# A retention layer's products with its state, in whole-array form and in four 64x64 tiles

## The chip, the cores and the metric

The kernel runs on one core of one Trainium2 chip. The metric is the time of one execution on the device in microseconds (us), as the median of several runs. A profile is taken of one more execution; it has its own span, from the first to the last instruction.

The engines of the core are named as in the profile: PE is TensorE (matrix products; PEld is its loading of weights, the operand that stays in the array), DVE is VectorE, ACT is ScalarE, POOL is GpSimd, SP is SyncE, which starts transfers. PE writes to PSUM alone, an accumulator memory of eight banks, each of 512 float32 in each of 128 partitions.

## The reference

Two layers follow each other. The first is a recurrent retention layer over `q`, `k`, `v` of 4 batches, 8 heads, 768 tokens and a head size of 64; its result, with the heads side by side, is `x` of 3072 tokens by 512. The second is a feed-forward layer with a snake activation.

```python
gamma = 1.0 - 2.0 ** (-5.0 - np.arange(H))
for t in range(S):
    state = gamma[None, :, None, None] * state + np.einsum('bhd,bhe->bhde', k[:, :, t], v[:, :, t])
    y[:, :, t] = scale * np.einsum('bhd,bhde->bhe', q[:, :, t], state)

h = x @ w_in                                  # 3072x512 by 512x2048
g = h + np.sin(alpha * h) ** 2 / (alpha + 1e-09)
out = g @ w_out                               # 2048x512
```

## The kernel before

**Chunks.** The recurrence is computed in chunks of 128 tokens, six for each batch, 24 in all (`order`; first the four first chunks of the batches, then the others batch by batch). With the decay folded into the values (`scale_v`) and into a factor at the exit (`qg`), a chunk `j` needs, for each head: the scores of its tokens with each other, masked (`scores`, the mask on DVE); the mix, masked scores times values; the product of the queries with the state that the earlier chunks left (`inter`); and the sum of keys times values over its tokens, which is added to the state.

**Wide chunks.** Chunks from the second batch's third on (`wide`, L86, 14 of them) are laid out in another way: 64 tokens of four heads in partitions 0 to 63, the same 64 tokens of the other four heads in partitions 64 to 127, and two such halves `f` of a chunk. `load_seq` (L89) loads them, one transfer a head, into `qk_seq` and `v_seq`, and SP turns queries and keys (`turn`, a transposing transfer) into `qkT`, where a pair of heads lies in the two halves of the partitions.

**A burst.** `burst(old, new, first)` (L398) puts the attention work of two chunks on PE in one go: `inter(old)`, `scores(new)`, `mix(old)` with the sums. The program is recorded in the order in which it is written, engine by engine; there is no scheduler. PE's matmuls are named in the profile with the part of the array that they use, rows * columns: 128*128 is the whole array, 64*64 a quarter. Row halves of a quarter tile belong to the partitions of the operands, column halves to the partitions of the output. In the code `tiles4` goes over the four pairs of halves (b, e).

- `inter` (L321 to 329): four matmuls in whole-array form. The state lies in `s_bd`, for each pair of heads a 128x128 matrix with the two heads' 64x64 states on its diagonal and zeros beside them. The results start two banks, `py[0]` (tag ps) and `py[1]` (tag ty).
- `scores` (L331 to 347): 16 quarter-tile matmuls, in four groups of four, into the two banks of `pa`, columns 0 to 383 of each; then DVE multiplies by the mask into `aTw`.
- `mix` (L349 to 358): 16 quarter-tile matmuls that add to `py`, columns 0 to 255.
- the sums (L359 to 369): 16 quarter-tile matmuls into columns 256 to 383 of `py`. At a batch's last chunk the sums are those of the next batch's first chunk instead (8 matmuls over 128 rows, 128*64), and after the very last chunk there are none.

What the banks hold is taken out one slot later: `leave` (L375, the exit, `py` times `qg` into `xT`), `keep` (L380, the sums added to the float32 state `s_f`) on DVE, and `hand` (L388), which copies `s_f` into the diagonal of the next chunk's `s_bd`, by two copies of 64 partitions, on ACT or (last batch) POOL. Two `s_bd` take turns.

**The feed-forward work around it.** `phase` (L545) goes through a group of two chunks in eight slots: eight matmuls of the hidden layer (L425, 256 columns), ACT's sine and square, then the attention work that is set for this slot, then four output matmuls of the group before (L450, 512 columns), then DVE's `gT` (L440). A burst stands in every fourth slot. PSUM's four banks with tag mm hold hidden and output sums.

**Before the wide chunks.** Chunks of the first batch and the first two of the second use `stage_A`, `stage_M`, `stage_S` with whole rows; `keep_S` (L283) copies the state from `ps` into `s_bd` on ACT. The state before the first wide chunk comes this way too, and `into_sum` (L719) copies it into `s_f` on DVE. `later_tables` (L189) makes the tables of decay for the wide layout at the start, from `lgq`, the heads' log decay by place.

Of the kernel before, what the change touches and what calls it, by code (L numbers as in the profile page):

```python
# [8 lines left out]
F32 = mybir.dt.float32  # L9
BF16 = mybir.dt.bfloat16  # L10
ACTF = mybir.ActivationFunctionType
ALU = mybir.AluOpType


@with_exitstack
def kernel(
# [15 lines left out]
    nc = tc.nc  # L32
    B, H, S, D = q.shape
    C = 128
    NCH = S // C
    NJ = B * NCH
    NP = H // 2
# [15 lines left out]
    place = {j: (g, i) for g, js in enumerate(groups) for i, j in enumerate(js)}  # L53

    consts = ctx.enter_context(tc.tile_pool(name="consts", bufs=1))
    big = ctx.enter_context(tc.tile_pool(name="big", bufs=1))
    work = ctx.enter_context(tc.tile_pool(name="work", bufs=2))
    psum = ctx.enter_context(tc.tile_pool(name="psum", bufs=1, space=bass.MemoryType.PSUM))
# [8 lines left out]
    raw = {}  # L67
# [18 lines left out]
    def wide(j):  # L86
        return j >= NCH + 2 and j % NCH > 0

    def load_seq(bt, names="qkv"):  # L89

        cs = [c for c in range(NCH) if wide(bt * NCH + c)]
        nh = 2 * len(cs)
        if "q" in names:
            raw["seq", bt] = (big.tile([128, nh, 2, NP, D], BF16, name=f"qk_seq{bt}"),
                              big.tile([128, nh, NP, D], BF16, name=f"v_seq{bt}"))
        tqk, tv = raw["seq", bt]
        for name, src in (("q", q), ("k", k), ("v", v)):
            if name not in names:
                continue
            for h in range(H):  # L100
                r = slice(64 * (h // NP), 64 * (h // NP) + 64)
                o = tv[r, :, h % NP, :] if name == "v" else tqk[r, :, "qk".index(name), h % NP, :]
                nc.gpsimd.dma_start(out=o, in_=src[bt, h, cs[0] * C:, :].rearrange("(f i) d -> i f d", i=64))  # L103
        for i, c in enumerate(cs):
            j, f = bt * NCH + c, slice(2 * i, 2 * i + 2)
            raw["qk", j], raw["k", j], raw["v", j] = tqk[:, f], tqk[:, f, 1], tv[:, f]
# [54 lines left out]
    lg = consts.tile([128, H], F32, name="lg")  # L161
# [24 lines left out]
    lgq = consts.tile([128, NP], F32, name="lgq")  # L186
    maskq = consts.tile([128, 192], BF16, name="maskq")

    def later_tables():  # L189
        for b in range(2):  # L190
            r = slice(64 * b, 64 * b + 64)
            for f in range(2):
                nc.vector.tensor_scalar_add(tok[r, :, f], pos[r, :], float(64 * (f - b)))
            nc.vector.tensor_copy(lgq[r], lg[r, NP * b:NP * b + NP])
        for f in range(2):
            nc.vector.tensor_mul(expoq[:, :, NP * f:NP * f + NP],
                                 tok[:, :, f, None].to_broadcast([128, NCH, NP]),
                                 lgq[:, None, :].to_broadcast([128, NCH, NP]))
# [20 lines left out]
    s_bd = [big.tile([128, NP, 128], BF16, name=f"s_bd{i}") for i in range(2)]  # L219


    s_f = big.tile([128, NP, D], F32, name="s_f")


    st = {}
# [46 lines left out]
    def stage_S(j):  # L272
# [7 lines left out]
                                 start=(c == 0 and p == 0), stop=True, skip_group_check=True)  # L280
        return ps

    def keep_S(j, ps):  # L283
        for e in range(2):
            r = slice(64 * e, 64 * e + 64)
            nc.scalar.copy(s_bd[(j % NCH + 1) % 2][r, :, r], ps[r, :, :])  # L286
# [29 lines left out]
    def half(x):  # L316
        return slice(64 * x, 64 * x + 64)

    tiles4 = [(b, e) for b in range(2) for e in range(2)]

    def inter(j):  # L321

        qkT, s = st["qkT", j], s_bd[j % NCH % 2]
        st["py", j] = [psum.tile([128, 512], F32, name=f"py{b}", tag=tag) for b, tag in enumerate(("ps", "ty"))]
        for m in range(2):
            for b in range(2):
                nc.tensor.matmul(st["py", j][b][:, m * 128:(m + 1) * 128].rearrange("p (f i) -> p f i", f=2),  # L327
                                 s[:, 2 * b + m, :], qkT[:, m:m + 5:4, half(b)],
                                 start=(m == 0), stop=True, skip_group_check=True)

    def scores(j):  # L331

        qkT = st["qkT", j]
        pa = psum.tile([128, 2, 512], F32, name="pa", tag="pa")
        for m in range(2):
            for b, e in tiles4:
                nc.tensor.matmul(pa[half(b), e, 192 * m:192 * m + 128].rearrange("p (f i) -> p f i", f=2),  # L337
                                 qkT[half(e), 2 + m, half(b)], qkT[half(e), m:m + 5:4, half(b)],
                                 start=(m == 0), stop=True, skip_group_check=True)
            for b, e in tiles4:  # L340
                nc.tensor.matmul(pa[half(b), e, 192 * m + 128:192 * m + 192],
                                 qkT[half(e), 6 + m, half(b)], qkT[half(e), 4 + m, half(b)],
                                 start=False, stop=True, skip_group_check=True)
        aT = work.tile([128, 2, 2, 192], BF16, name="aTw", tag="aT", bufs=2)
        st["aT", j] = aT
        return {"mask": lambda: nc.vector.tensor_mul(aT, pa[:, :, 0:384].rearrange("p e (m t) -> p e m t", m=2),  # L346
                                                     maskq[:, None, None, :].to_broadcast([128, 2, 2, 192]))}

    def mix(j, first=None):  # L349

        py, aT, vs, c = st["py", j], st["aT", j], raw["v", j], j % NCH
        for m in range(2):
            for b, e in tiles4:
                nc.tensor.matmul(py[b][half(e), m * 128:(m + 1) * 128], vs[half(b), 0, 2 * m + e, :],  # L354
                                 aT[half(b), e, m, 0:128], start=False, stop=True, skip_group_check=True)
            for b, e in tiles4:
                nc.tensor.matmul(py[b][half(e), m * 128 + 64:(m + 1) * 128], vs[half(b), 1, 2 * m + e, :],
                                 aT[half(b), e, m, 128:192], start=False, stop=True, skip_group_check=True)
        now = j if c < NCH - 1 else first  # L359
        if now is not None:  # L360
            ks, vs = raw["k", now], raw["v", now]
            for f in range(2 if wide(now) else 1):
                for m in range(2):
                    for b, e in tiles4:
                        h = 4 * b + 2 * m + e
                        nc.tensor.matmul(py[b][half(e), 256 + 64 * m:320 + 64 * m],  # L366
                                         ks[half(b), f, 2 * m + e, :] if wide(now) else ks[:, h, :],
                                         vs[half(b), f, 2 * m + e, :] if wide(now) else vs[:, h, :],
                                         start=False, stop=True, skip_group_check=True)
        g, i = place[j]  # L370
        if g not in xT:
            xT[g] = work.tile([128, KS, sizes[g] * C], BF16, name="xT", tag="xT", bufs=3)
        x = xT[g][:, :, i * C:(i + 1) * C]

        def leave():  # L375
            for b in range(2):
                nc.vector.tensor_mul(x[:, 2 * b:2 * b + 2, :], py[b][:, 0:256].rearrange("p (m t) -> p m t", m=2),  # L377
                                     qg[:, c, 2 * b:2 * b + 2])

        def keep():  # L380
            for b in range(2):
                o, new = s_f[:, 2 * b:2 * b + 2], py[b][:, 256:384].rearrange("p (m d) -> p m d", m=2)
                if wide(now):
                    nc.vector.tensor_add(o, o, new)  # L384
                else:
                    nc.vector.tensor_copy(o, new)

        def hand():  # L388
            for e in range(2):
                copy = nc.gpsimd.tensor_copy if now // NCH == 3 else nc.scalar.copy  # L390
                copy(s_bd[(now % NCH + 1) % 2][half(e), :, half(e)], s_f[half(e)])  # L391

        more = {"exit": leave}
        if now is not None:
            more.update(keep=keep, hand=hand)
        return more

    def burst(old, new, first=None):  # L398

        inter(old)  # L400
        return {**(scores(new) if new is not None else {}), **mix(old, first)}

    def run(more, *kinds):
        for kind in kinds:
# [196 lines left out]
    b = early(1)  # L601
# [3 lines left out]
    c = early(3)  # L605
    a.sq("A")
    b.add()
    b = early(4, "ps")
# [8 lines left out]
    c = early(6)  # L617
    a.sq("A")
    b = early(7)
# [15 lines left out]
    b = Slot(0, 4, (n3, n4), 4)  # L635
# [4 lines left out]
    b = Slot(0, 10)  # L640
# [5 lines left out]
    b = Slot(0, 12)  # L646
# [5 lines left out]
    b = Slot(0, 14)  # L652
# [57 lines left out]
    for g in range(2, NG - 1):  # L710
        first = P.index(groups[g + 1][0])
# [5 lines left out]
        atts[place[0]].setdefault(place[1], []).append(fn)  # L717

    def into_sum():  # L719
        nc.vector.tensor_copy(s_f, st["ps"])  # L720

    def M_last(j):
        stage_M(j)
# [8 lines left out]
    for n in range(6, NJ + 1):  # L732
        new = P[n] if n < NJ else None
        first = new - 1 if n < NJ and new % NCH == 1 else None
# [46 lines left out]
```

## Time and profile before

| | |
|---|---|
| median of 3 runs | 214.4 us (214.4 to 214.45) |
| span of the profiled execution | 213.0 us |
| PE busy | 201.3 us, 94% of the span |
| PEld busy | 134.3 us, 63% |
| DVE busy | 155.1 us, 73% |
| ACT busy | 160.4 us, 75% |
| POOL busy | 107.2 us, 50% |
| granted clock of PE | 1.000 |

The page of the profile lists busy time, a chain of the work that ended last, followed back from the last instruction, and groups of instructions by line. A group's row has engine, operation, output <- inputs, the part of the array for PE, the shapes, how often, busy time in us and mean ns of one, and then the idle time of the engine just before them with what ended it. The timeline and the chain in order of time have the start and the length in us in their first two columns; instructions of one kind that follow each other are one row with their count. PE's matmuls are pipelined: several are in flight, and the length of one is its latency. "issue" is time in which an engine waited for nothing that the profile shows.

### The profile page before, as it was taken

The page shows a single profiled execution, that of the slowest core. Times are in us where ns is not written, and L with a number is a line of the kernel's source. Part 1 is how long each engine was busy: PE and PEld are TensorE (multiplying, and loading weights), DVE is VectorE, ACT ScalarE, POOL GpSimd, SP SyncE. Part 2 cuts the span into 40 slices and gives each one's busy share as a digit, 9 for nine tenths or more (in the row PEclk, how much of TensorE's full clock was granted, in tenths as well). Part 3 has the DMA queues.
Part 4 walks back from the last instruction along what each step waited for, and adds up shares of the span by engine and source line. Part 5 has one row for each costly group of instructions (what it writes and reads, how often), then busy time and mean ns, then how long its engine had stood idle before and what let it go on. Part 6 is the DMA issues. An engine that isn't in the chain of part 4 may idle for free.

```text
span 213.0 us, 5482 instructions
## 1 busy us (share of the span) xinstructions
PE 201.3 (94%) x2171; PEld 134.3 (63%) x2197; DVE 155.1 (73%) x349; ACT 160.4 (75%) x346; POOL 107.2 (50%) x145
## 2 busy tenths in 40 slices
PE   7898899899989999999999999999999999999994
PEld 3445554456766766766767667667667667666654
DVE  4877849876996678678678777777877877666550
ACT  7588696758887877977977977977876876788821
POOL 8976333787989729999789941001231131000000
DMA  9999999999998999999999994407403100110112
GB/s 128 155 196 187 206 207 170 149 114 241 142 158 74 147 160 150 159 103 152 167 151 170 150 145 104 98 3 98 103 12 91 51 30 23 52 49 0 52 49 99
DMA packets 101337, 25.00 MB, mean 117 GB/s; under 512 B 93872, under 2 KB 98368, under 8 KB 101312
## 3 DMA queue, kind: packets, MB, share of 16 engines
q0 software_dynamic: 77504, 13.38, 88.4%
q1 hardware_dynamic: 23664, 11.22, 27.0%
q8 instruction: 17, 0.28, 0.6%
q14 instruction: 8, 0.07, 0.1%
q10 hardware_dynamic: 144, 0.07, 0.1%
HBM read 27.27 MB, written 6.29 MB: 158 GB/s over the span
## 4 chain that ended last, share of the span: by engine, by line
PE 72%; DMA 13%; DVE 7%; POOL 5%; issue 2%; POOLq 0%
PE po L450 32%; PE ph L425 30%; DMA qkr<-in_k_dram 8%; DMA w_in<-in_moe_w_in_dram 4%; DVE gT L440 3%; DVE aT L269 2%; POOL qkr L83 2%; PE poh L475 2%; PE pa L337 2%; PE py L327 1%; POOL vr L83 1%; PE py L366 1%; PE py L354 1%; POOL w_out L116 1%; PE py L299 1%
## 5 line engine op out<-in xcount | busy, mean ns | idle before, releaser
L440 DVE SCALAR_TENSOR_TENSOR gT<-s,rec_alpha,ph 128x256 bf16<-128x256 f32 (+3 forms) x184 | 82.3, 488 | 37.8 <-ACT s L433 37.5
L428 ACT ACTIVATE s<-ph,alpha_sb 128x256 f32<-128x256 f32 (+3 forms) x184 | 79.1, 479 | 33.3 <-PE ph L425 31.7
L425 PE MATMUL ph<-xT,w_in 128*128 128x256 bf16 (+3 forms) x735 | 98.6, 277 | 0.3 <-DVE gT L440 0.2
L450 PE MATMUL po<-w_out,gT 128*128 128x512 bf16 x344 | 90.5, 380 | 4.3 <-issue 3.3
L425 PEld LDWEIGHTS <-w_in 128*128 128x128 bf16 x736 | 70.5, 98 | 30.7 <-issue 1.0
L433 ACT ACTIVATE s<-s 128x512 f32<-128x512 f32 (+1 forms) x92 | 57.1, 621 | 2.5
L450 PEld LDWEIGHTS <-gT 128*128 128x128 bf16 x368 | 33.8, 98 | 27.0 <-issue 1.2
L391 POOL CAST s_bd<-s_f 64x256 bf16<-64x256 f32 x10 | 3.9, 394 | 41.8 <-DVE s_f L384 23.6
L137 POOL TENSOR_TENSOR v_seq<-v_seq,kgq 128x512 bf16<-128x512 bf16 x14 | 14.7, 1081 | 10.5 <-ACT s L433 5.5
L103 POOL DMA_DIRECT2D qk_seq<-in_q_dram x24 | 17.1, 755 | 3.5 <-DMA v_seq<-in_v_dram 1.9
L103 POOL DMA_DIRECT2D qk_seq<-in_k_dram x24 | 17.0, 745 | 0.9 <-DMA qk_seq<-in_q_dram 0.5
L462 DVE COPY o_sb<-po 128x512 f32<-128x512 f32 x19 | 13.1, 691 | 5.4 <-PE po L450 5.4
L103 POOL DMA_DIRECT2D v_seq<-in_v_dram x24 | 17.0, 772 | 0.0
L346 DVE TENSOR_TENSOR aTw<-pa,maskq 128x768 bf16<-128x768 f32 x14 | 13.3, 950 | 0.0
L83 POOL DMA_DIRECT2D vr<-in_v_dram x10 | 9.2, 924 | 5.0 <-DMA w_in<-in_moe_w_in_dram 1.7
L494 PE MATMUL spare<-warm 128*128 128x512 bf16 x27 | 9.9, 492 | 1.3 <-DVE warm L156 1.2
L377 DVE TENSOR_TENSOR xT<-py,qg 128x256 bf16<-128x256 f32 x28 | 10.5, 416 | 0.0
L83 POOL DMA_DIRECT2D qkr<-in_q_dram x9 | 8.1, 902 | 3.7 <-DMA w_out<-in_moe_w_out_dram 1.6
L83 POOL DMA_DIRECT2D qkr<-in_k_dram x9 | 8.1, 897 | 3.7 <-DMA w_out<-in_moe_w_out_dram 3.3
L137 POOL TENSOR_TENSOR vr<-vr,kg 128x512 bf16<-128x512 bf16 x7 | 7.5, 1081 | 1.1 <-DMA vr<-in_v_dram 1.1
L269 DVE TENSOR_TENSOR aT<-pa,mask 128x1024 bf16<-128x1024 f32 x6 | 7.3, 1219 | 0.7 <-PE pa L265 0.7
L286 ACT CAST s_bd<-ps 64x256 bf16<-64x256 f32 x14 | 5.1, 361 | 2.3 <-PE ps L279 2.2
(93 smaller groups left out, 154.7 us busy)
## 6 DMA issues: line engine op xcount, KB each, us to landing
out_dram<-o_sb SPq DMA_DIRECT2D x23, 256.0 KB, 2.8
w_in<-in_moe_w_in_dram POOLq DMA_DIRECT2D x4, 512.0 KB, 10.6
w_out<-in_moe_w_out_dram POOLq DMA_DIRECT2D x4, 512.0 KB, 14.6
vr<-in_v_dram POOLq DMA_DIRECT2D x10, 128.0 KB, 6.5
qk_seq<-in_q_dram POOLq DMA_DIRECT2D x16, 80.0 KB, 6.3
qk_seq<-in_k_dram POOLq DMA_DIRECT2D x16, 80.0 KB, 4.6
v_seq<-in_v_dram POOLq DMA_DIRECT2D x16, 80.0 KB, 5.9
qkr<-in_q_dram POOLq DMA_DIRECT2D x9, 128.0 KB, 7.1
```

Source lines behind the costliest of these rows:

```text
L83: nc.gpsimd.dma_start(out=t, in_=chunk_of(src, j))
L103: nc.gpsimd.dma_start(out=o, in_=src[bt, h, cs[0] * C:, :].rearrange("(f i) d -> i f d", i=64))
L137: eng.tensor_mul(t, t, by[:, j % NCH, :, None].to_broadcast([128, H, D]))
L269: nc.vector.tensor_mul(aT.rearrange("p e n t -> p (e n) t"), pa.rearrange("p e n t -> p (e n) t"), m)
L346: return {"mask": lambda: nc.vector.tensor_mul(aT, pa[:, :, 0:384].rearrange("p e (m t) -> p e m t", m=2), maskq[:, None, None, :].to_broa ...
L377: nc.vector.tensor_mul(x[:, 2 * b:2 * b + 2, :], py[b][:, 0:256].rearrange("p (m t) -> p m t", m=2), qg[:, c, 2 * b:2 * b + 2])
L425: nc.tensor.matmul(self.ph[:, m, :], w_in[:, i, f * 128:(f + 1) * 128], xT[g][:, i, self.lo:self.hi], start=(m == 0 and i == 0), stop=(i = ...
L428: nc.scalar.activation(out=self.s[:, m, :], in_=self.ph[:, m, :], func=ACTF.Sin, scale=alpha_sb[:, f:f + 1])
L433: nc.scalar.activation(out=self.s, in_=self.s, func=ACTF.Square)
L440: nc.vector.scalar_tensor_tensor(gT[self.g][:, f, self.lo:self.hi], self.s[:, m, :], rec_alpha[:, f:f + 1], self.ph[:, m, :], op0=ALU.mult ...
L450: nc.tensor.matmul(po[g, ts], gT[g][:, f, ts * C:(ts + 1) * C], w_out[:, f, :], start=(f == 0), stop=(f == FF - 1))
L462: nc.vector.tensor_copy(o_sb, po[g, ts])
```

## The change

Two things change for the wide chunks.

First, `inter` uses quarter tiles. The state lies in `s_q`, without zeros: `s_q` has, in partition half e and place 2b + m, the state of one head. To let the eight products of a burst fall on four different tiles, the heads of the second half (4 to 7) are swapped in pairs (`spot`): in the loads, in the table `lgq`, in the output halves of `inter` and `mix` (`half(e ^ b)`) and in `sums`. `hand` becomes one copy of 128 partitions. Where the state comes from the old layout, `turned` copies it with the halves of heads 4 to 7 exchanged, by three copies.

Second, the sums of a chunk go ahead of the mix and into columns 384 to 511 of the scores' banks `pa`, where the next burst has scores (11 of 14 bursts). At the two batch borders they stay behind the mix in `py`. Ahead of the mix stands a wait for the last product of `inter`, written as a no-op with a dependency; in the built program the wait is on the mix's first weight load, or on an instruction of its own before it at the two batch borders, where that load has another wait already. PE's program has 112 instructions more (eight for each burst); ACT has 7 copies fewer, POOL 5 fewer, DVE 4 more.

```diff
+AFTER = mybir.DependencyInfo(mybir.DependencyClass.Sync, mybir.DependencyReason.DATA)
...
+    def spot(h):
+        return h // NP, (h % NP) ^ (h // NP)
...
             for h in range(H):
-                r = slice(64 * (h // NP), 64 * (h // NP) + 64)
-                o = tv[r, :, h % NP, :] if name == "v" else tqk[r, :, "qk".index(name), h % NP, :]
+                b, at = spot(h)
+                r = slice(64 * b, 64 * b + 64)
+                o = tv[r, :, at, :] if name == "v" else tqk[r, :, "qk".index(name), at, :]
...
-            nc.vector.tensor_copy(lgq[r], lg[r, NP * b:NP * b + NP])
+            for e in range(2):
+                nc.vector.tensor_copy(lgq[r, e::2], lg[r, NP * b + (e ^ b):NP * b + NP:2])
...
+    s_q = [big.tile([128, NP, D], BF16, name=f"s_q{i}") for i in range(2)]
...
+    def turned(to, ps, copy):
+        copy(to[:, 0:2], ps[:, 0:2])
+        for e in range(2):
+            copy(to[64 * e:64 * e + 64, 2:4], ps[64 - 64 * e:128 - 64 * e, 2:4])
+
     def keep_S(j, ps):
+        if wide(j + 1):
+            turned(s_q[(j % NCH + 1) % 2], ps, nc.scalar.copy)
+            return
...
     def inter(j):
-        qkT, s = st["qkT", j], s_bd[j % NCH % 2]
+        qkT, s = st["qkT", j], s_q[j % NCH % 2]
...
         for m in range(2):
-            for b in range(2):
-                nc.tensor.matmul(st["py", j][b][:, m * 128:(m + 1) * 128].rearrange("p (f i) -> p f i", f=2),
-                                 s[:, 2 * b + m, :], qkT[:, m:m + 5:4, half(b)],
-                                 start=(m == 0), stop=True, skip_group_check=True)
+            for b, e in tiles4:
+                last = nc.tensor.matmul(st["py", j][b][half(e ^ b), m * 128:(m + 1) * 128].rearrange("p (f i) -> p f i", f=2),
+                                        s[half(e), 2 * b + m, :], qkT[half(e), m:m + 5:4, half(b)],
+                                        start=(m == 0), stop=True, skip_group_check=True)
+        return last
...
+    def sums(now, to, lo):
+        ks, vs = raw["k", now], raw["v", now]
+        for f in range(2 if wide(now) else 1):
+            for m in range(2):
+                for b, e in tiles4:
+                    h = 4 * b + 2 * m + (e ^ b)
+                    nc.tensor.matmul(to[b][half(e), lo + 64 * m:lo + 64 + 64 * m],
+                                     ks[half(b), f, 2 * m + e, :] if wide(now) else ks[:, h, :],
+                                     vs[half(b), f, 2 * m + e, :] if wide(now) else vs[:, h, :],
+                                     start=False, stop=True, skip_group_check=True)
+
+    def mix(j, behind):
+        n = nc.tensor.nop()
+        tc.add_manual_dep(n.ins, behind.ins.name, AFTER)
+        py, aT, vs = st["py", j], st["aT", j], raw["v", j]
         for m in range(2):
...
+            for f in range(2):
+                for b, e in tiles4:
+                    nc.tensor.matmul(py[b][half(e ^ b), m * 128 + 64 * f:(m + 1) * 128], vs[half(b), f, 2 * m + e, :],
+                                     aT[half(b), e, m, 128 * f:128 + 64 * f],
+                                     start=False, stop=True, skip_group_check=True)
+
+    def burst(old, new, first=None):
+        c = old % NCH
+        behind = inter(old)
+        more = scores(new) if new is not None else {}
+        now = old if c < NCH - 1 else first
+        at = None
+        if now is old:
+            pa = st["pa", new]
+            at = [pa[:, b, 384:512] for b in range(2)]
+            sums(now, [pa[:, b] for b in range(2)], 384)
+        mix(old, behind)
+        py = st["py", old]
+        if now is not None and now is not old:
+            at = [py[b][:, 256:384] for b in range(2)]
+            sums(now, py, 256)
...
         def hand():
-            for e in range(2):
-                copy = nc.gpsimd.tensor_copy if now // NCH == 3 else nc.scalar.copy
-                copy(s_bd[(now % NCH + 1) % 2][half(e), :, half(e)], s_f[half(e)])
+            copy = nc.gpsimd.tensor_copy if now // NCH == 3 else nc.scalar.copy
+            copy(s_q[(now % NCH + 1) % 2], s_f)
...
     def into_sum():
-        nc.vector.tensor_copy(s_f, st["ps"])
+        turned(s_f, st["ps"], nc.vector.tensor_copy)
```

More of the change, by code (lines that the diff above doesn't have):

```diff
@@ L321, in inter @@
     def inter(j):
-        qkT, s = st["qkT", j], s_bd[j % NCH % 2]
+        qkT, s = st["qkT", j], s_q[j % NCH % 2]
         st["py", j] = [psum.tile([128, 512], F32, name=f"py{b}", tag=tag) for b, tag in enumerate(("ps", "ty"))]
         for m in range(2):
-            for b in range(2):
-                nc.tensor.matmul(st["py", j][b][:, m * 128:(m + 1) * 128].rearrange("p (f i) -> p f i", f=2),
-                                 s[:, 2 * b + m, :], qkT[:, m:m + 5:4, half(b)],
-                                 start=(m == 0), stop=True, skip_group_check=True)
+            for b, e in tiles4:
[3 more added lines that the diff above has]
+        return last
     def scores(j):
         qkT = st["qkT", j]
-        pa = psum.tile([128, 2, 512], F32, name="pa", tag="pa")
+        pa = st["pa", j] = psum.tile([128, 2, 512], F32, name="pa", tag="pa")
         for m in range(2):
@@ L347, in scores @@
                                                      maskq[:, None, None, :].to_broadcast([128, 2, 2, 192]))}
-    def mix(j, first=None):
-        py, aT, vs, c = st["py", j], st["aT", j], raw["v", j], j % NCH
-        for m in range(2):
[L353 to L370, printed above, removed]
@@ new lines, in burst @@
+    def burst(old, new, first=None):
[13 more added lines that the diff above has]
+            sums(now, py, 256)
+        g, i = place[old]
@@ L381, in keep @@
             for b in range(2):
-                o, new = s_f[:, 2 * b:2 * b + 2], py[b][:, 256:384].rearrange("p (m d) -> p m d", m=2)
+                o, add = s_f[:, 2 * b:2 * b + 2], at[b].rearrange("p (m d) -> p m d", m=2)
                 if wide(now):
-                    nc.vector.tensor_add(o, o, new)
+                    nc.vector.tensor_add(o, o, add)
                 else:
-                    nc.vector.tensor_copy(o, new)
+                    nc.vector.tensor_copy(o, add)
         def hand():
-            for e in range(2):
-                copy = nc.gpsimd.tensor_copy if now // NCH == 3 else nc.scalar.copy
-                copy(s_bd[(now % NCH + 1) % 2][half(e), :, half(e)], s_f[half(e)])
-        more = {"exit": leave}
+            copy = nc.gpsimd.tensor_copy if now // NCH == 3 else nc.scalar.copy
+            copy(s_q[(now % NCH + 1) % 2], s_f)
+        more["exit"] = leave
         if now is not None:
@@ L396, in mix @@
         return more
-    def burst(old, new, first=None):
-        inter(old)
-        return {**(scores(new) if new is not None else {}), **mix(old, first)}
     def run(more, *kinds):
```

## The prediction

> **What bounds the kernel now.** I read the page first (span, busy shares, the chain that ended last), then the windows view by stage, then the chain of waits in order of time, and last the timeline of TensorE around one attention burst.
>
> ```profile
> span 213.0 us, 5482 instructions
> PE 72%; DMA 13%; DVE 7%; POOL 5%; issue 2%; POOLq 0%
> ...
> 81.00:186.00 105.00, 102.78 (x1305) 72.97 (x1318) 79.60 (x185) 82.90 (x176) 50.97 (x71) 1.00 1.06 101
> ```
>
> The first row is the span; the second the shares of the chain. The windows row is the stage that holds the attention bursts; after the window and its length come the busy times of PE, PEld, DVE, ACT and POOL, then the clock. TensorE is busy for 102.78 of 105.0 us at clock 1.00, while DVE has 25.4 us and ACT 22.1 us to spare.
>
> ```profile
> 82.60 0.81 PE po L450 x3
> ...
> 90.47 0.81 PE po L450 x3
> ...
> 98.35 0.81 PE po L450 x3
> ...
> 106.34 0.81 PE po L450 x3
> ...
> 177.33 0.81 PE po L450 x3
> ...
> 184.90 0.81 PE po L450 x3
> ```
>
> These are the chain's pieces right behind bursts. The chain stays on PE from one to the next, 7.87 to 7.88 us apart, 7.99 us over the first batch border (98.35 to 106.34) and 7.57 us before the last burst. What a burst takes on PE is therefore paid in full, and what it saves should arrive in full at the end.
>
> ```profile
> 81.02 0.60 PE L425 MATMUL ph<-xT,w_in 128*128 128x256 bf16 x4
> 81.45 0.39 PE L327 MATMUL py<-qkT,s_bd 128*128 128x128 bf16 x4
> 81.77 0.25 PE L337 MATMUL pa<-qkT 64*64 64x128 bf16 x4
> 81.85 0.20 PE L341 MATMUL pa<-qkT 64*64 64x64 bf16 x4
> 81.88 0.23 PE L337 MATMUL pa<-qkT 64*64 64x128 bf16 x4
> 81.94 0.20 PE L341 MATMUL pa<-qkT 64*64 64x64 bf16 x4
> 81.97 0.23 PE L354 MATMUL py<-aTw,v_seq 64*64 64x128 bf16 x4
> 82.03 0.20 PE L357 MATMUL py<-aTw,v_seq 64*64 64x64 bf16 x4
> 82.05 0.23 PE L354 MATMUL py<-aTw,v_seq 64*64 64x128 bf16 x4
> 82.11 0.20 PE L357 MATMUL py<-aTw,v_seq 64*64 64x64 bf16 x4
> 82.14 0.30 PE L366 MATMUL py<-v_seq,qk_seq 64*64 64x64 bf16 x16
> 82.60 0.59 PE L450 MATMUL po<-w_out,gT 128*128 128x512 bf16 x2 [0.16 <-issue]
> ...
> L327 PE MATMUL py<-qkT,s_bd 128*128 128x128 bf16 x56 | 5.4, 220 | 0.0
> ...
> L366 PE MATMUL py<-v_seq,qk_seq 64*64 64x64 bf16 x176 | 3.3, 193 | 0.0
> L366 PE MATMUL py<-vr,qkr 128*64 128x64 bf16 x16 | 0.6, 202 | 0.0
> ```
>
> One burst, by starts (64*64 is a quarter of the array, 128*128 the whole); the "duration" of a matmul (220 ns in the group row) is its pipelined latency, so a price is the distance of starts. The reader should see: the four whole-array products of L327 last 0.39 us together, the last starts 0.39 - 0.22 = 0.17 later than the first, so 0.056 apart. From that last start (81.62) to the first quarter tile (81.77) are 0.15, that is 0.056 for the product and 0.093 for the change from whole array to quarters. From there a group of four quarter tiles runs as one: 0.06 with 128 columns (81.88 to 81.94), 0.03 with 64 (81.94 to 81.97), 0.087 a pair. The first group behind the change costs 0.08 (81.77 to 81.85), 0.02 more. The 16 sums last 0.30 - 0.19 = 0.11 from first start to last, 0.032 a group of four, 0.13 in all.
>
> The counts give the bursts: 56/4 = 14, of them 176/16 = 11 with sums in quarters (regular), 16/8 = 2 at batch borders with sums over 128 rows, and 1 last without sums or scores.
>
> **The change, part by part.** *State product.* Four whole-array products (4 x 0.056 = 0.223) become eight 64x64 ones, two groups of four with 128 columns. By the scores' groups these cost 0.059 each, 0.118. The 0.093 is only moved: the array now changes to quarters at the hidden-layer product before the burst. A change from there is in the trace:
>
> ```profile
> 72.54 1.04 PE L425 MATMUL ph<-xT,w_in 128*128 128x256 bf16 x8
> 73.50 0.41 PE L299 MATMUL py<-qkT,s_bd 128*64 128x128 bf16 x8
> ```
>
> The last of the eight starts at 73.58 - 0.273 = 73.31 and would be followed at its spacing of (0.60 - 0.273)/3 = 0.109 at 73.42; the next starts at 73.50, 0.08 to 0.09 on. The surcharge of 0.02 moves along too. So a burst gets 0.223 - 0.118 = 0.105 shorter, if a group of this product runs like one of the scores.
>
> No row shows quarter tiles of different row halves that write one bank at the same time, as the new product does: tile (b, e) reads rows half e and writes bank b, half e^b. Bounds for a group: below, 0.053, the pace of 16 scores at 0.087 a pair spread by columns (0.087 x 128/192 = 0.058, less a rounding of 0.005); above, 0.223, four one after another at 0.056. I take 0.059, as the operand shapes, the four distinct tiles and the order of row halves are those of the scores; the banks alone differ.
>
> The Trainium skill, TensorEngine Tiling (Array Packing), section Gotcha 1: PSUM Pressure, says that different row tiles cannot access the same PSUM bank simultaneously. By that the two row halves would have to take turns; what this would make of the time is the first rival. The skill's page PSUM — Partial Sum Buffer, section PSUM bank collisions raise a hardware error, draws the line at one bank and one 32-partition quadrant, and by that the halves here would not meet and a group stays at 0.06. No run here shows either yet.
>
> *The wait ahead of the mix.* The first weight load of the mix now waits for the last state product (both write the same quarter of a bank, from different row halves). Behind it in PE's order stand the rest of the mix and the next output products, so a stall here is paid. Let T be the last state product's start. It completes at T + 0.22. Two rows bound the way from there:
>
> ```profile
> 81.66 0.84 ACT L428 ACTIVATE s<-ph,alpha_sb 128x256 f32<-128x256 f32 x2 [0.24 <-PE ph L425]
> ...
> 8.70 1.22 DVE L269 TENSOR_TENSOR aT<-pa,dec 128x1024 bf16<-128x1024 f32 x1
> ...
> 9.96 0.41 PE L303 MATMUL py<-aT,vr 128*64 128x128 bf16 x8 [0.83 <-DVE aT L269]
> ```
>
> ACT starts 0.04 after PE's product ends (81.02 + 0.60 = 81.62), PE 0.04 after DVE ends (9.92). So the load may go at T + 0.26 to T + 0.30 (once or twice the 0.04). Without the wait, the mix would start at T + 0.05 + 2 x 0.087 (scores) + 0.13 (sums, now ahead of it) = T + 0.35. In 11 bursts the cover is 0.05 to 0.09, and I take 0; if a load that could not be pulled ahead costs 0.05 more than that, up to 0.03 a burst, 0.3 us in all. If the sums were not there, the mix would be due at T + 0.22. That is the case in the 2 border bursts, where the sums stay behind it: a stall of 0.04 to 0.13; I take 0.10 and the gain is gone. In the last burst nothing stands between; the mix is due at T + 0.05 and starts at T + 0.26 to 0.30, a stall of 0.21 to 0.25. Against the 0.105 gained there, it loses about 0.14 net.
>
> *Sums moved.* Same 16 instructions in both places, in one array mode, 0. The mask on DVE now waits for the sums' end, as scores and sums report together: with the first quarter tile at 81.345 + 0.109 + 0.093 = 81.55, scores at 81.69 and sums from 81.86, their last starts at 81.97 and ends at 82.16, plus 0.04.
>
> ```profile
> 82.24 0.95 DVE L346 TENSOR_TENSOR aTw<-pa,maskq 128x768 bf16<-128x768 f32 x1
> ```
>
> The mask started at 82.24 as DVE was busy before it; so 0. Without that cover it costs DVE some 0.02 a burst, still inside its spare time. The additions into the running state read the scores' banks one slot later, and the next scores need these 7.9 us later: 0.
>
> *Copies.* Handing on the state is one copy instead of two (ACT or POOL), 0.39 less a burst on engines that wait; 0. The first state of the first wide batch takes 3 copies instead of 2 on ACT and 3 instead of 1 on DVE, once, near 75 us:
>
> ```profile
> 75.78 0.42 DVE L720 COPY s_f<-ps 128x256 f32<-128x256 f32 x1 [0.89 <-ACT s_bd L286]
> ...
> 7.90 0.57 DVE L194 COPY lgq<-lg 64x4 f32<-64x4 f32 x1
> ...
> 38.57 0.40 PE L246 MATMUL pt<-ident,qkr 128*128 128x128 bf16 x4 [0.50 <-DMA qkr<-in_k_dram]
> ```
>
> That is about 0.4 more on DVE, where 0.89 idle stand before; what is late next is the mask and two hidden-layer sums, one slot of 1.74 us ahead of need; 0, up to 0.3. Two more small copies on DVE at the start (0.57 each at worst, 0.1 to 0.2 by their neighbours) run down the start's chain, but PE idles 0.50 for a load at 38.57: 0, at worst 0.6. The loads are the same in number, size and queue; only heads' places differ.
>
> *Sum* against the profiled span of 213.0: 11 x (-0.105) = -1.16; 2 x (-0.105 + 0.10) = -0.01; last +0.14; the rest 0. Together -1.03, a span of 212.0. The median lies 1.4 above the profiled span (214.4), so 213.4 us. With stalls of 0.03 and late DVE work it is 213.8 (+0.33 and some of the start); with groups of 0.053 and no stall at borders 213.0.
>
> **The rivals.** *Row halves take turns in a bank* (slower). Place: the two groups of the state product. A group takes two passes, 0.059 more each, 0.118 a burst, 14 x 0.118 = 1.65: -1.03 + 1.65 = +0.62, 215.0 us. It decides from 0.074 a burst (1.03/14), so even a partial turn of 0.037 a group eats the gain. For it: no row has this pattern. Against: the halves of the bank that are written at one time are different partitions. Four in a row, 0.223 a group, would give 14 x 0.33 = 4.6 more, 218 us; I leave this outside.
>
> *The mix waits for all before it, not for the state product alone* (slower). If the wait lets go only once scores and sums have left the array, the mix starts at their last start + 0.193 + 0.04 in place of + 0.03: 0.20 in each of 11 bursts, +2.2, 215.6 us. For it: a wait of PE on its own latest product is new here. Against: the wait names the state product's count, and waits already met cost nothing in the burst shown (0.087 a pair right through).
>
> *The gain is taken elsewhere* (no change, 214.4). ACT or DVE would have to end last. Against: in this stage PE's own rows show 0.16 of issue at each burst and no wait for another engine; the bursts ask for only 1.3% more pace from engines that are 76% and 79% busy.
>
> **How the numbers follow.** Forecast 0.68 (own range 213.0 to 213.8), turns in a bank 0.10, wait for all 0.09, gain taken elsewhere 0.08, the start or another cost large enough to undo it 0.05. A measurement here can tell 0.2%, 0.43 us. The forecast is faster nearly whole (0.67), and 0.01 of the rest too; the case of no change with parts of the first rival and the start gives 0.14; slower has 0.18. The range goes from 212.9 (a little faster in groups and borders) to 214.7, over the case of no change; it leaves out the two slower rivals, 0.19.
>
> **What would show it.** In the profile after: the same-place distance between bursts 7.77 where it was 7.87; the state product as x8 with its last start 0.07 after its first; the first mix product some 0.03 behind the last sums, no idle PE there. A gap ahead of the mix speaks for the second rival, state groups of 0.1 or more for the first, a hidden-layer product that waits for DVE for the third. The start is right if the transposes at 38.6 still wait for their load. I am wrong if the distance of bursts does not shrink by 0.08 to 0.12.

## The result and the profile after

The changed kernel takes 213.5 us (median of 5 runs), against 214.4 us for the kernel before on the same chip. The ratio is 0.9959 with a 95% interval of 0.9942 to 0.9976, so it is faster by 0.2 to 0.6%; the forecast of 213.4 us lies 0.1 us from the median.

The page of the changed kernel, its windows view of the same stage, and its chain of waits in order of time, at the pieces right behind the first four bursts and the last two:

```profile
span 211.7 us, 5581 instructions
...
PE 78%; DVE 14%; ACT 4%; issue 3%; ACTq 0%
```

```profile
81.00:186.00 105.00, 102.70 (x1366) 70.66 (x1378) 81.50 (x188) 80.43 (x170) 47.30 (x63) 1.00 0.99 100
```

```profile
82.11 0.81 PE po L481 x3
...
89.88 0.81 PE po L481 x3
...
97.64 0.81 PE po L481 x3
...
105.71 0.81 PE po L481 x3
...
175.88 0.81 PE po L481 x3
...
183.61 0.81 PE po L481 x3
```

PE is as busy as before and at the same clock; it does the same work in less time. The distances are read as before: 7.77 between regular bursts (before 7.87), but 8.07 over the batch border (97.64 to 105.71; before 7.99), and 7.73 in front of the last burst (before 7.57). So 11 bursts gain, three lose.

The timeline of PE around the first burst, for the rows that were shown of before:

```profile
80.75 0.49 PE L456 MATMUL ph<-xT,w_in 128*128 128x256 bf16 x3
81.17 0.31 PE L344 MATMUL py<-qkT,s_q 64*64 64x128 bf16 x8
81.31 0.23 PE L355 MATMUL pa<-qkT 64*64 64x128 bf16 x4
81.37 0.20 PE L359 MATMUL pa<-qkT 64*64 64x64 bf16 x4
81.39 0.23 PE L355 MATMUL pa<-qkT 64*64 64x128 bf16 x4
81.45 0.20 PE L359 MATMUL pa<-qkT 64*64 64x64 bf16 x4
81.48 0.30 PE L374 MATMUL pa<-v_seq,qk_seq 64*64 64x64 bf16 x16
81.61 0.34 PE L387 MATMUL py<-aTw,v_seq 64*64 64x128 bf16 x16
82.11 0.81 PE L481 MATMUL po<-w_out,gT 128*128 128x512 bf16 x3 [0.16 <-issue]
```

The eight state products take 0.14 from their first start (81.17) to the scores' (81.31): 0.08 for the first group behind the change of array form, 0.06 for the second; the last of them starts 0.31 - 0.22 = 0.09 behind the first. In the kernel before, 0.32 went by from the whole-array products' first start (81.45) to the scores' (81.77), the 0.093 of the change between them included; now this stands in front of 81.17. The sums end where the mix begins (0.13 after their start), with no gap.

The three bursts that lose have no sums there. First the batch border, then the last burst, in the same view:

```profile
104.47 0.31 PE L344 MATMUL py<-qkT,s_q 64*64 64x128 bf16 x8
...
104.74 0.20 PE L359 MATMUL pa<-qkT 64*64 64x64 bf16 x4
104.94 0.37 PE L387 MATMUL py<-aTw,v_seq 64*64 64x128 bf16 x16
...
182.70 0.31 PE L344 MATMUL py<-qkT,s_q 64*64 64x128 bf16 x8
183.08 0.37 PE L387 MATMUL py<-aTw,v_seq 64*64 64x128 bf16 x16
```

A product's latency being 0.22, the last state product starts at 104.47 + 0.31 - 0.22 = 104.56 and the mix 0.38 behind it, though the scores' last group was started at 104.74 and is followed within 0.03 elsewhere. In the last burst it is 182.79 and 183.08, 0.29.

Where the time came from: 11 x (-0.11) + 2 x 0.075 + 0.16 = -0.90 us, which is the difference of the medians. The profiled spans differ by more, 1.3 us, and the rest was there before the first burst: 82.60 against 82.11. A second profile of the kernel before (r1, below) tells how.

### The profile page after: what moved, and what is told of

It is laid out like the page before. It is cut to its first block, busy times and chain, and to the rows that moved or that the text cites. A ratio compares the mean times of both kernels' runs of the same rounds, so it can differ in the third digit from the quotient of the medians.

```text
span 211.7 us, 5581 instructions
## 1 busy us (share of the span) xinstructions
PE 199.4 (94%) x2227; PEld 131.0 (62%) x2253; DVE 155.7 (74%) x353; ACT 157.7 (74%) x339; POOL 105.2 (50%) x140
## 4 chain that ended last, share of the span: by engine, by line
PE 78%; DVE 14%; ACT 4%; issue 3%; ACTq 0%
PE po L481 33%; PE ph L456 31%; DVE gT L471 5%; DVE aT L277 4%; PE spare L525 3%; ACT s L459 2%; ACT s L464 2%; PE poh L506 2%; PE py L344 2%; PE py L387 1%; DVE s L466 1%; PE pa L273 1%; PE pa L355 1%; PE py L320 1%; PE pa L374 1%
## 5 line engine op out<-in xcount | busy, mean ns | idle before, releaser
L427 POOL CAST s_q<-s_f 128x256 bf16<-128x256 f32 x5 | 2.0, 397 | 43.3 <-DVE s_f L421 25.7
L525 PE MATMUL spare<-warm 128*128 128x512 bf16 x27 | 9.2, 464 | 1.3 <-DVE warm L162 1.2
L277 DVE TENSOR_TENSOR aT<-pa,dec 128x1024 bf16<-128x1024 f32 x4 | 4.9, 1223 | 1.8 <-PE pa L273 1.8
```

The lines of the kernel that those rows point to most:

```text
L277: nc.vector.tensor_mul(aT.rearrange("p e n t -> p (e n) t"), pa.rearrange("p e n t -> p (e n) t"), m)
L525: nc.tensor.matmul(spare["ps"], warm[:, :128], warm, start=True, stop=True)
```

## The experiments

All ran on chips beside runs of the kernel before (medians 214.3 to 214.4 us); e9, r1 and r2 are one execution each. Their "distance" is that between the output products behind two bursts, in the chain of waits.

**e1: quarter tiles, the sums left behind the mix.**

```diff
-        if now is old:
-            pa = st["pa", new]
-            at = [pa[:, b, 384:512] for b in range(2)]
-            sums(now, [pa[:, b] for b in range(2)], 384)
         mix(old, behind)
         py = st["py", old]
-        if now is not None and now is not old:
+        if now is not None:
             at = [py[b][:, 256:384] for b in range(2)]
```

> The quarter-tile state product alone, the sums left behind the mix. Theory (the gain of 0.11 us a burst is there only while the sums cover the mix's wait): the mix stalls behind the scores in all 13 bursts with scores as it does at the batch borders of the changed kernel, by about 0.16 us; the distance of regular bursts is 7.765 + 0.16 = 7.93 us (before 7.87, changed 7.77), and 11 x 0.06 + 2 x 0.08 + 0.16 = 1.0 us more than before: 215.3 us. Rival (moving the sums is incidental, the wait is covered by the scores): distance 7.77 us, 213.5 us.

Measured: 215.14 us, ratio to before 1.0037 (1.0015 to 1.0059): half the change is slower than none of it. Its chain of waits has distances of 7.94 to 7.95 up to the first burst of the last batch (7.90 ahead of the first bursts of the two batches before it), and 7.85 to 7.86 from there:

```profile
82.26 0.81 PE po L477 x3
...
90.21 0.81 PE po L477 x3
...
161.82 0.81 PE po L477 x3
...
169.68 0.81 PE po L477 x3
```

The two kinds have each their row in PE's timeline (first a burst of the first wide batch, then one of the last):

```profile
89.08 0.31 PE L344 MATMUL py<-qkT,s_q 64*64 64x128 bf16 x8
...
89.36 0.20 PE L359 MATMUL pa<-qkT 64*64 64x64 bf16 x4
89.55 0.34 PE L387 MATMUL py<-aTw,v_seq 64*64 64x128 bf16 x13
...
168.65 0.31 PE L344 MATMUL py<-qkT,s_q 64*64 64x128 bf16 x8
...
168.93 0.20 PE L359 MATMUL pa<-qkT 64*64 64x64 bf16 x4
169.03 0.37 PE L387 MATMUL py<-aTw,v_seq 64*64 64x128 bf16 x16
```

By the same sum, the mix starts 0.38 behind the last state product in the one (89.17 to 89.55) and 0.29 in the other (168.74 to 169.03). In the built program the mix's first weight load waits for POOL too (the scaled values) in the first two batches, and for a transfer in the last one's first burst, and the wait for the state product then stands in an instruction of its own. In the two bursts with 7.90 that instruction has a second wait, for a transfer, and the mix starts 0.34 behind the last state product (113.13 to 113.47 in the second of them); why sooner than 0.38 stays open. Later in the last batch POOL has handed on the state, the state product has waited for POOL already, and the load carries the one wait itself. The scores alone cover neither. Against the changed kernel the uncovered wait costs 7.95 - 7.77 = 0.18, or 0.09 where it is on the load.

**e2: the sums moved ahead, everything else as before.** Whole-array state product, no wait, heads not swapped:

```diff
+        now = j if c < NCH - 1 else first
+        at = None
+        if now is j:
+            pa = st["pa", new]
+            at = [pa[:, b, 384:512] for b in range(2)]
+            sums(now, [pa[:, b] for b in range(2)], 384)
...
+        if now is not None and now is not j:
+            at = [py[b][:, 256:384] for b in range(2)]
+            sums(now, py, 256)
```

> The sums alone moved ahead of the mix into the scores' banks; state product in whole-array form and heads as before, no wait. Theory (the order of quarter-tile products costs nothing): distance of regular bursts 7.87 us, 214.4 us within 0.2. Rival (part of the gain comes from the earlier sums, by what DVE can start earlier or by the gap behind the burst): a distance of 7.82 us or less, 213.9 us or less.

Measured: 214.42 us, ratio 1.001 (0.9993 to 1.0026), distances of 7.87 to 7.88 between regular bursts. The order alone is worth nothing that these runs show. With e1 this makes the two halves of the change one: the quarter tiles bring the gain, and the moved sums keep the wait from taking it back.

**e7: the wait named later.** The sums return their last product, and in regular bursts the mix waits for that:

```diff
-            sums(now, [pa[:, b] for b in range(2)], 384)
+            behind = sums(now, [pa[:, b] for b in range(2)], 384)
```

> The changed kernel, but in the 11 regular bursts the wait ahead of the mix names the last sum in place of the last state product, so nothing covers it. Theory (the wait holds the mix until the named product has left the array, its last start + 0.19 + some 0.07 to 0.1): the mix's start moves from 0.03 to 0.18 to 0.26 us behind the last sums, distance 7.92 to 8.0, time 213.5 + 1.7 to 2.5 = 215.2 to 216.0 us. Rival (a wait of PE on itself is met by PE's own order and costs nothing): 213.5 us.

Measured: 216.94 us, ratio 1.0128 (1.0104 to 1.0152); distances 8.03 to 8.04 between regular bursts, 0.27 to 0.28 above the changed kernel, a little over the upper expectation. PE's timeline of its second burst:

```profile
90.25 0.30 PE L374 MATMUL pa<-v_seq,qk_seq 64*64 64x64 bf16 x16
90.64 0.37 PE L388 MATMUL py<-aTw,v_seq 64*64 64x128 bf16 x16
```

The last sum starts at 90.25 + 0.30 - 0.19 = 90.36 and leaves at 90.55; the mix starts 0.09 later, 0.28 behind the start in place of 0.02. The first group of the mix then costs 0.08 in place of 0.06, as it does behind the pause at a border of the changed kernel. 11 x 0.275 is 3.0 of the 3.4 us more. In the profiled execution (217.25 us) the output products behind the first burst come at 83.12, 1.0 us later than the changed kernel's. Of this, 0.66 is a start that was late in that execution: PE waits 0.62 us for a load of `w_in` ahead of its products at 16.61, which start at 15.97 in the changed kernel's profile. The other 0.35 is the first burst's own; its mix starts 0.35 behind the last sum in place of 0.28, and why stays open. The two fastest of the four runs, 216.57 and 216.62 us, lie 3.1 above the changed kernel, so the bursts account for them; that a late start makes the rest of the median's surplus is likely, but not shown for the runs without a profile.

**e5: the state products issued twice.** The state's part of the result is doubled.

```diff
-        for m in range(2):
+        for m, again in ((0, 0), (1, 0), (0, 1), (1, 1)):
             for b, e in tiles4:
...
-                                        start=(m == 0), stop=True, skip_group_check=True)
+                                        start=(m == 0 and not again), stop=True, skip_group_check=True)
```

> The changed kernel with the eight state products of each burst issued twice (the state's part of the result is doubled). Theory (PE is the bound, a group of four costs 0.056 us): 0.112 us more in each of 14 bursts, distance 7.88 us, +1.57, 215.1 us. If row halves took turns in a bank: 0.2 or more a burst, 216.3 us or more. If PE were not the bound: 213.5 us.

Measured: 215.05 us, ratio 1.004 (1.0025 to 1.0055), 1.55 above the changed kernel; distances 7.87 to 7.88. Timeline of PE, first burst:

```profile
82.29 0.42 PE L344 MATMUL py<-qkT,s_q 64*64 64x128 bf16 x16
82.54 0.23 PE L355 MATMUL pa<-qkT 64*64 64x128 bf16 x4
```

From first product to scores 0.25, with 16 products, against 0.14 with 8: two groups more for 0.11, 0.055 each. This is the price of a group by itself, and no more than a whole-array product with the same 128 columns (0.056). Both that price and PE as the bound are confirmed: 14 x 0.11 = 1.54.

**e3: whole-array products in the three bursts without cover.** A third, zero-filled state `s_x` takes the heads so that they leave in the swapped halves; no wait in these bursts, as none was there before:

```diff
+        if j % NCH == NCH - 1:
+            for m in range(2):
+                for b in range(2):
+                    nc.tensor.matmul(st["py", j][b][:, m * 128:(m + 1) * 128].rearrange("p (f i) -> p f i", f=2),
+                                     s_x[:, 2 * b + m, :], qkT[:, m:m + 5:4, half(b)],
+                                     start=(m == 0), stop=True, skip_group_check=True)
+            return None
...
+            if now % NCH == NCH - 2:
+                for e in range(2):
+                    copy(s_x[half(e), 0:2, half(e)], s_f[half(e), 0:2])
+                    copy(s_x[half(e), 2:4, half(1 - e)], s_f[half(e), 2:4])
+                return
```

> The changed kernel with the whole-array state product (a zero-filled state with the halves of heads 4 to 7 exchanged) in the three bursts that have no sums ahead of the mix, and no wait there. Theory (in those three the wait costs more than the quarter tiles bring): the distances over the borders return to 7.99 us (changed: 8.07) and the one before the last output products to 7.57 (changed: 7.73), 0.31 us in all, 213.2 us; regular bursts stay at 7.765. Rival (the four copies that fill the zero-filled state delay something, or the difference lies elsewhere at the borders): 213.5 us or more.

Measured: 213.34 us, ratio to before 0.9963 (0.9941 to 0.9984). The distances are those expected; the chain at the border and at the last two bursts:

```profile
97.65 0.81 PE po L495 x3
...
105.64 0.81 PE po L495 x3
...
175.74 0.81 PE po L495 x3
...
183.31 0.81 PE po L495 x3
```

7.99 and 7.57, as in the kernel before, with 7.76 to 7.77 elsewhere. From the first burst to the last output products shown it is 0.3 us shorter than the changed kernel in the profile (116.82 against 117.13, from 82.12 to 198.94 and from 82.11 to 199.24). The runs can't tell the two apart: the intervals overlap nearly whole.

**e9: one wait less at the border.** A single 64x64 product that reads the values takes the wait for POOL ahead of the mix:

```diff
+        if first is not None:
+            v0 = raw["v", old][half(0), 0, 0, :]
+            nc.tensor.matmul(st["py", old][0][half(0), 448:512], v0, v0, start=False, stop=True, skip_group_check=True)
```

> The changed kernel with one small extra product at the two batch borders that reads the values ahead of the mix, so that the mix's first weight load has the wait for the state product alone and no instruction of its own for it. Theory (the border stalls longer than forecast, as the wait stands in an instruction of its own): the mix starts 0.29 us behind the last state product as in the last burst (changed: 0.39), the distance over a border is 7.97 to 8.0 us. Rival (the wait itself takes 0.39 there): 8.07 us or more.

Timeline of PE at the first border:

```profile
104.48 0.31 PE L344 MATMUL py<-qkT,s_q 64*64 64x128 bf16 x8
...
104.79 0.19 PE L399 MATMUL py<-v_seq 64*64 64x64 bf16 x1
104.86 0.37 PE L387 MATMUL py<-aTw,v_seq 64*64 64x128 bf16 x16
```

The mix starts at 104.86, 0.29 behind the last state product (104.57), and the distance is 7.97 and 7.98 at the two borders, where it was 8.06 to 8.07. One product more made the border 0.08 to 0.1 us shorter. The one execution took 213.34 us, which by itself can't be told from the changed kernel's runs (212.77 to 213.85).

**r1 and r2: both kernels profiled once more, unchanged.**

> The kernel before, unchanged, for a second profile. Theory (of the 1.3 us between the profiled spans 0.9 come from the bursts, and 0.4 from when one load of keys landed in those two executions): bursts 7.87 us apart as before; the first burst's output products may come earlier or later than at 82.60 us. Rival (the start differs by the program): they come at 82.6 us again.

> The changed kernel, unchanged, for a second profile. Theory (the start depends on the execution): bursts 7.765 us apart, the first burst's output products not necessarily at 82.11 us. Rival (the start differs by the program): at 82.1 us again, with no wait for a load near 38 us.

The second profile of the kernel before, its span, the output products behind its first two bursts and the transposes that had waited at 38.57:

```profile
span 212.7 us, 5482 instructions
```

```profile
82.23 0.81 PE po L450 x3
...
90.11 0.81 PE po L450 x3
```

```profile
37.70 0.61 PE L246 MATMUL pt<-ident,qkr 128*128 128x128 bf16 x8
38.15 1.03 PE L425 MATMUL ph<-xT,w_in 128*128 128x512 bf16 x4
```

This execution does not wait for the load of keys at all: the eight transposes run through, and the first burst is 0.37 us earlier than in the profile that the prediction was made from. Its time, 214.44 us, is that of the median. The changed kernel's second profile has 82.12 and no such wait either, with a time of 213.51; by itself that is what r2's rival had expected, and it is r1 that decides. Between executions without the late load the first burst's products move by 0.11 to 0.12 (82.23 to 82.11 or 82.12), which is that burst's own gain. So the start does not differ by the program, and 0.4 of the 1.3 us between the first two spans was the late load. The forecast's sign for the start, transposes that still wait at 38.6, did not show in either profile of the changed kernel; by r1 it belongs to the execution.

## Why the prediction was right, step by step

**PE is the bound.** Shown both ways: what a burst lost (0.11) and what was added to it (e5, 0.11) came out in the distance of bursts, and in the medians.

**State product, -0.105 a burst.** Measured -0.108 to -0.11: the second group takes 0.056, not 0.059. The change of array form was only moved, as forecast: 0.20 from the last hidden-layer product's start (80.75 + 0.49 - 0.27 = 80.97) to the first quarter tile (81.17), 0.109 of it that product's spacing.

**Row halves that write one bank at one time.** The value taken from the scores held; the first rival (turns, 0.118 more a burst) is out by the burst after and by e5's 0.055 for a group. The Trainium skill, TensorEngine Tiling (Array Packing), section Gotcha 1: PSUM Pressure, says that different row tiles cannot access the same PSUM bank simultaneously; two row halves in one bank took no turns here (0.055 to 0.056 a group), and the measurement decides. The line that the Trainium skill draws in PSUM — Partial Sum Buffer, section PSUM bank collisions raise a hardware error, at one bank and one 32-partition quadrant, agrees with that time. Whether the results would be spoiled without the wait, where the quarters do meet, wasn't tried.

**The wait, regular bursts.** Forecast: let go at T + 0.26 to 0.30, needed at T + 0.35, no stall. The bursts after show no gap, e1 shows the load's wait at 0.29, inside the bounds. The second rival is out: the wait named the state product, and only where it was made to name the sums (e7) did the mix wait for them. Its price was put at 0.20 a burst and is 0.275.

**The wait, borders and last burst.** This is the term that was mis-sized. The border stall was forecast as 0.04 to 0.13, taken as 0.10, with nothing lost; it was 0.16 to 0.17 (0.38 in place of 0.22). With 0.02 more for the mix's first group behind the pause, which the forecast did not count, less the gain of 0.11, each border lost 0.07 to 0.08. The step that failed is the bound "once or twice the 0.04" for the way from the product's end to the load: it holds for a wait on the load, and at the border the wait has an instruction of its own, which takes about 0.1 more. e9 shows it by taking that instruction away, e1 by having both kinds in one kernel. The last burst lost 0.16, forecast 0.14. In the sum the borders are 0.16 worse than forecast and the last burst 0.02, the regular bursts 0.05 better: 0.13 in all, from -1.03 to -0.90.

**Sums, mask, copies.** Zero, as forecast: e2 for the order. For the late copies, DVE's timeline of the second profile of the kernel before (r1), whose start had no late load either, and of the changed kernel:

```profile
75.42 0.42 DVE L720 COPY s_f<-ps 128x256 f32<-128x256 f32 x1 [0.90 <-ACT s_bd L286]
75.76 0.95 DVE L346 TENSOR_TENSOR aTw<-pa,maskq 128x768 bf16<-128x768 f32 x1
```

```profile
75.49 0.29 DVE L293 COPY s_f<-ps 128x128 f32<-128x128 f32 x1 [0.98 <-ACT s_q L295]
75.82 0.59 DVE L295 COPY s_f<-ps 64x128 f32<-64x128 f32 x2
76.44 0.96 DVE L364 TENSOR_TENSOR aTw<-pa,maskq 128x768 bf16<-128x768 f32 x1
```

The mask starts 0.68 later (75.76 to 76.44): 0.07 from ACT's copies and 0.61 from DVE's own, forecast about 0.4. The first burst is on time all the same, so the zero holds with a larger delay than was allowed for. The two more copies at the start cost nothing that shows.

**From the span to the median.** The span of 213.0 held 0.37 us of a late load, which the second profile with the median's time doesn't have. So the 1.4 us from that span to the median are too few by as much: it is 1.74 to 1.8 in the others (214.44 - 212.7, 213.5 - 211.7). As only a difference was taken from the sum, the two errors cancel in the forecast.

## What to carry to other kernels

Small products in four tiles paid here because they replaced a zero-filled whole-array form, whose one product costs PE as much as a group of four. But the gain of 0.1 us a burst was smaller than the wait that the new form brought, and only other products in front of the waiting one kept it. Count what stands between a product and one that waits for it: in this case it took 0.29 us from the start of a 128-column product, 0.38 where the wait got an instruction of its own (0.34 in two bursts of e1). Where there is no such work, the old form was the better one by the profile (e3, 0.3 us, which the runs don't resolve), and where a second wait makes that instruction, an earlier product can take it (e9).

## What the runs showed of the hardware that was not expected

Behind a wait of PE for its own product, set on the weight load, the next product starts 0.07 to 0.09 us after the trace has the awaited one leave the array (0.29 from its start with a latency of 0.22; in e7 0.28 with 0.19, but 0.35 in its first burst); with the wait in an instruction of its own ahead of the load it is 0.16 (0.38 with 0.22; 0.34 in two bursts of e1). A group of four quarter tiles that write two banks, each from two row halves at once, takes 0.055 to 0.056 us for 128 columns, what one whole-array product takes.
